# Where a batch's loads stand in the DMA queue: behind the stage's last store, with turns ahead of v

## The chip, the cores and the metric

The kernel runs on one core of one Trainium2 chip. The metric is device time in microseconds for one execution, inputs and outputs in HBM; the figure of a kernel is the median of several runs.

The names used below: TensorE (PE) does the matmuls, VectorE (DVE), ScalarE (ACT) and GpSimd (POOL) work element by element, SP only issues DMAs. Each engine works through its own program in order.

## The reference, cut to what matters

Attention over 8 batches, 8 heads, 576 positions, 64 dims, then a gated feed-forward block. Heads 0 to 3 ("plain") see the last 32 positions, heads 4 to 7 ("dilated") every fourth of the last 128.

```
scores = q @ k.T / sqrt(64)                 # per batch and head
plain:   0 <= i - j < 32
dilated: 0 <= i - j < 128 and (i - j) % 4 == 0
attn = softmax(scores where the mask holds)
x = (attn @ v), heads side by side          # 4608 tokens x 512
out = (gelu(x @ w_gate) * (x @ w_val)) @ w_out   # 512 -> 1536 -> 512
```

## The kernel before

**Tiles.** The 4608 tokens are cut into 9 chunks of 512. A chunk c has a gate stage (12 blocks of 128 hidden columns; a block is 4 matmuls with `wg` and 4 with `wv`, line 638) and an output stage (4 blocks of 128 tokens, 12 matmuls each, line 645). All these matmuls are 128x128 by 512 columns. Attention is spread between them: each batch has four pairs of heads, numbered n = 4 b to 4 b + 3, two plain and two dilated. Batches 2 and 3 begin with the dilated pairs, all others with the plain ones (`pair`).

**Lists of places.** The order on TensorE, and with it that on ScalarE and VectorE, is written out by hand, as words in the dictionaries `gates`, `outs` and `firsts`. A number is so many feed-forward matmuls. S is a pair's scores, P the exponential (ScalarE, line 510), M its mask (VectorE, 515), D the denominators, N the numerators (line 459 or 448), A or T and B the reciprocal (ScalarE 608 and 610, or VectorE 599 to 616), X the product that writes `xT` (VectorE, 629). `N22@1+D23@0` emits the two as one, split over quarters of the array (`emit_tiles`). The digit after @ is the PSUM window. `g` and `u` are a gate block's activation (803) and product (808). `e3@0` evicts block 3 of chunk 0 to an `osb` buffer on ScalarE (656) and stores it (660). `firsts` orders the first 16 matmuls of the gate stage.

**Loads.** A batch from 2 on is loaded in two steps on SP's queue. `load_first` (word F) brings q and k in float32 to the three parts of `stage`, and GpSimd casts them to `s16` (lines 221, 233). `load_rest` (word H) turns them by transposing DMAs into `qp`, `qd` and `dense` (line 275, "turns"), brings v to parts 1 and 2 of `stage`, and GpSimd spreads the keys out of `dense` (283, 291), copies the rest of q (L330) and casts v (264). Part 1 holds first k's plain heads, then v's plain heads; part 2 q's dilated heads, then v's dilated heads. A DMA that reuses a part waits for the cast that read it.

SP's program, in the order of the code, is therefore a row of loads with the stores between them. F2 and H2 stand in chunk 0's output list, and R (H3, F4, H4) in chunk 2's gate list. The others are issued by the loop at the end of the code: F3 ahead of chunk 1, F5 and H5 ahead of chunk 3, F6 and H6 ahead of chunk 4, F7 and H7 ahead of chunk 5. The word `e3@(c-1)`, the last store of a chunk's output, stands early in the next chunk's gate list, so on SP it is behind these loads. There are four `osb` buffers (`osbp`, bufs=4); block 3 of one chunk takes the buffer of block 3 of the chunk before.

The order of the transfers inside H:

```
turn qp; turn kdp (plain k)
load_v plain            # 4 transfers of 144 KB
turn qd; turn kdd (dilated k)
load_v dilated          # 4 of 128 KB and 4 of 16 KB
GpSimd: spread plain k, cast plain v, spread dilated k, copy rest of q, cast dilated v
```

Of the kernel before, what the change touches and what calls it, by code (L numbers as in the profile page):

```python
# [21 lines left out]
def kernel(  # L22
# [11 lines left out]
    B, H, S, D = q.shape  # L34
# [128 lines left out]
    def gated(ins):  # L163

        if "dma" in gate:
            tc.add_manual_dep(ins.ins, gate.pop("dma").ins.name, SYNC, reason="order of loads")
# [41 lines left out]
    def st_of(i):  # L208
        return stage[:, 1280 * i : 1280 * i + 1280]

    def load_plain(src, b, i):
        st = st_of(i).rearrange("p (k h d) -> p k h d", k=5, h=HK)
        for kb in range(4):
            nc.sync.dma_start(out=st[:, kb], in_=src[b, 0:HK, kb * P : kb * P + P, :].rearrange("h p d -> p h d"))
        for x in range(2):
            rest = src[b, x * HK : x * HK + HK, S - 64 : S, :].rearrange("h p d -> p h d")
            nc.sync.dma_start(out=st[64 * x : 64 * x + 64, 4], in_=rest)

    def cast_plain(t, i):
        for g in range(2):  # L220
            nc.gpsimd.tensor_copy(  # L221
                s16[:, 1280 * t + 640 * g : 1280 * t + 640 * g + 640].rearrange("p (k c) -> p k c", k=5),
                st_of(i).rearrange("p (k g c) -> p k g c", k=5, g=2)[:, :, g],
            )

    def load_dil(src, b, i):
        rows_ = src[b, HK:H, 0 : 4 * P, :].rearrange("h (p r) d -> p h (r d)", r=4)
        nc.sync.dma_start(out=st_of(i)[:, 0:1024].rearrange("p (h c) -> p h c", h=HK), in_=rows_)
# [9 lines left out]
    def load_v(b, i, plain):  # L238

        st = st_of(i)  # L240
        for g in range(2 * plain):
            for x in range(2):
                rows_ = v[b, 2 * g + x].rearrange("(j p) d -> p j d", p=64)
                dst = st[half_of(x, b and g), 576 * g : 576 * g + 576].rearrange("p (j d) -> p j d", j=NB2)
                gated(nc.sync.dma_start(out=dst, in_=rows_))  # L245
        for g in range(2 - 2 * plain):
            for x in range(2):
                half = st[half_of(x, g), 576 * x : 576 * x + 512]
                rows_ = v[b, HK + 2 * g + x, 0 : 4 * P].rearrange("(i p r) d -> p i (r d)", i=2, r=4)
                nc.sync.dma_start(out=half.rearrange("p (i c) -> p i c", i=2), in_=rows_)  # L250
        for g in range(2 - 2 * plain):
            for x in range(2):
                at = slice(576 * x + 512, 576 * x + 576)
                nc.sync.dma_start(out=st[half_of(x, g), at], in_=v[b, HK + 2 * g + x, S - 64 : S])

    def cast_v(dst, i, gs=(0, 1), swap=1, plain=1):

        st = st_of(i)[:, 0:1152].rearrange("p (e d) -> p e d", d=D)
        for g in gs:
            for x in range(2):  # L260
                y = x ^ (g * swap)
                src = g if plain else y
                at, of = (slice(NB2 * i, NB2 * i + NB2) for i in (g, src))
                nc.gpsimd.tensor_copy(dst[half_of(x), at, half_of(y)], st[half_of(x), of])  # L264

    def half_of(x, swap=0):
        y = x ^ (1 if swap else 0)
        return slice(64 * y, 64 * y + 64)
# [5 lines left out]
    def turn(dst, src):  # L274
        nc.sync.dma_start_transpose(out=dst, in_=src)
# [17 lines left out]
    def load_first(b):  # L293
        load_plain(q, b, 0)
        load_plain(k, b, 1)
        load_dil(q, b, 2)
        cast_plain(0, 0)
        cast_plain(1, 1)
        load_dil(k, b, 0)
        cast_dil(0, 2)  # L300
        cast_dil(1, 0)
# [17 lines left out]
    def load_rest(b):  # L319
        qp, qd, kp, kd, vp, vd = tiles["two", b] = views(b)  # L320
        turn(qp.rearrange("p g (k c) -> p (g k) c", c=P), s16[:, 0:1280])
        turn(kdp.rearrange("p g (k c) -> p (g k) c", c=P), s16[:, 1280:2560])
        load_v(b, 1, True)
        turn(qd.rearrange("p g r i -> p (g r) i")[:, :, 0:P], s16[:, 2560:3584])
        turn(kdd.rearrange("p g r i -> p (g r) i")[:, :, 0:P], s16[:, 3584:4608])
        load_v(b, 2, False)
        spread_plain(kp)
        cast_v(vp, 1)
        spread_dil(kd, kdp[:, :, S:640])
        nc.gpsimd.tensor_copy(qd[:, :, :, P:NCL], qp[:, :, S:640].rearrange("p g (i r) -> p g r i", r=4))  # L330
        cast_v(vd, 2, plain=0)

    def v_first(g):

# [449 lines left out]
    def run_program(c, words, mms, banks):  # L784
# [3 lines left out]
        for word in words.split():  # L788
# [47 lines left out]
            "u8 2 t9@5@0 t11@7@0 6 g9 u9 2 t12@4@1 t14@6@1 6 g10 u10 2 t13@5@1 t15@7@0 6 g11 u11"  # L836
        ),
        1: (
            "4 N7@0 e3@0 1 X7 1 G 8 g0 2 g1 1 u0 2 u1 2 g2 4 u2 4 g3 4 u3 4 g4 4 u4 4 g5 4 u5 4 g6 4 u6 4 g7 4 u7 "
            "4 g8 4 u8 4 g9 4 u9 4 g10 4 u10 4 g11 3"  # L840
        ),
        2: (
            "4 N11@1 e3@1 R 1 X11 G 7 g0 3 g1 u0 3 u1 3 g2 4 u2 4 g3 4 u3 4 g4 4 u4 4 g5 4 u5 4 g6 4 u6 4 g7 4 u7 "
            "4 g8 4 u8 4 g9 4 u9 4 g10 4 u10 4 g11 3"
        ),
        3: (
            "4 N15@0 e3@2 1 X15 G 7 g0 3 g1 u0 3 u1 3 g2 4 u2 4 g3 4 u3 4 g4 4 u4 4 g5 4 u5 4 g6 4 u6 4 g7 4 u7 4 "
            "g8 4 u8 4 g9 4 u9 4 g10 4 u10 4 g11 3"
        ),
        4: (  # L850
            "3 e3@3 M21 1 N19@0+D20@1 G 1 X19 6 T20 3 g0 2 N20@0+D21@1 g1 u0 1 u1 3 B20 1 g2 4 u2 3 T21 1 g3 4 u3 "
            "N21@1 1 X20 3 g4 1 B21 4 u4 3 X21 g5 4 u5 4 g6 4 u6 4 g7 4 u7 4 g8 4 u8 4 g9 4 u9 4 g10 4 u10 4 g11 "
            "3"
        ),
        5: (
            "G 2 N24@1 2 B24 e3@4 2 g0 2 X24 3 u0 2 g1 4 u1 4 g2 4 u2 4 g3 4 u3 4 g4 4 u4 4 g5 4 u5 4 g6 4 u6 4 "
            "g7 4 u7 4 g8 4 u8 4 g9 4 u9 4 g10 4 u10 4 g11 3"
        ),
        6: (
            "G 3 T28 3 e3@5 1 M31 N28@0+D29@1 g0 1 B28 4 u0 1 g1 1 T29 5 u1 N29@1 1 X28 1 g2 3 B29 4 u2 1 g3 2 "  # L860
            "X29 3 u3 3 g4 4 u4 4 g5 4 u5 4 g6 4 u6 4 g7 4 u7 4 g8 4 u8 4 g9 4 u9 4 g10 4 u10 4 g11 3"
        ),
        7: (
            "G 6 e3@6 2 g0 3 u0 2 g1 4 u1 4 g2 4 u2 4 g3 4 u3 4 g4 4 u4 4 g5 4 u5 4 g6 4 u6 4 g7 4 u7 4 g8 4 u8 4 "
# [2 lines left out]
    }  # L867
    outs = {
        0: (
            "V1 F2 S4@4 E P4 11 M4 S5@2 1 P5 3 D4@0 M5 S6@2 1 T4 P6 5 M6 e0@0 S7@2 1 P7 1 B4 3 e1@0 H2 1 M7 7 "  # L870
            "N4@1+D5@0 1 A5 X4 5 N5@0+D6@1 e2@0 1 A6 X5 5 N6@1+D7@0 1 A7 X6 1"
        ),
        1: (
            "1 u11 5 S8@0 1 E P8 10 e0@1 M8 1 S9@0 1 P9 3 D8@1 M9 S10@0 1 T8 P10 4 e1@1 1 M10 N8@0+D9@1 S11@0 B8 "
            "A9 3 X8 2 P11 4 e2@1 1 M11 N9@1+D10@0 1 A10 X9 7 N10@0+D11@1 1 A11 X10 1"
        ),
        2: (
            "1 u11 5 S12@2 1 E P12 10 e0@2 M12 1 S13@2 1 P13 3 D12@0 M13 S14@2 1 T12 P14 4 e1@2 1 M14 N12@1+D13@0 "
            "S15@2 B12 A13 3 X12 2 P15 4 e2@2 1 M15 N13@0+D14@1 1 A14 X13 7 N14@1+D15@0 1 A15 X14 1"
        ),  # L880
        3: (
            "1 u11 5 S16@0 1 E P16 10 e0@3 1 M16 S17@0 1 P17 3 D16@1 M17 S18@0 A16 4 N16@0+D17@1 e1@3 1 P18 X16 3 "
            "A17 1 M18 S19@0 3 P19 2 N17@0+D18@1 e2@3 M19 S20@0 A18 1 X17 4 P20 1 N18@1+D19@0 1 M20 A19 S21@0 1 "
            "X18 3 P21 1"
        ),
        4: (
            "1 u11 5 S22@2 1 E P22 10 e0@4 M22 1 S23@2 1 P23 3 D22@0 M23 S24@2 A22 4 N22@1+D23@0 e1@4 1 P24 X22 5 "
            "S25@2 T23 1 P25 N23@1 2 M24 2 e2@4 1 B23 3 M25 D24@0 2 X23 5 T24"
        ),
        5: (  # L890
            "D25@0 u11 2 T25 3 N25@1+S26@0 B25 1 E P26 3 X25 7 e0@5 M26 1 S27@0 1 P27 3 D26@0 M27 S28@0 1 T26 P28 "
            "4 e1@5 1 M28 N26@1+D27@0 S29@0 B26 1 P29 2 T27 4 N27@0+S30@0 X26 1 P30 3 B27 1 e2@5 1 D28@1+S31@0 "
            "M29 1 P31 1 M30 3 X27 3"
        ),
        6: "D30@0 u11 1 E A30 5 N30@1+D31@0 1 T31 5 X30 N31@0 e0@6 4 B31 4 X31 5 e1@6 12 e2@6 11",
    }
    firsts = {
        0: "000 100 002 102 001 101 010 110 012 112 011 111 003 103 013 113",
        1: "000 001 010 011 002 012 100 101 102 110 111 112 003 013 103 113",
        2: "002 003 012 013 000 010 102 103 100 112 001 011 101 113 110 111",  # L900
        3: "002 003 012 013 000 010 102 103 100 112 001 011 101 113 110 111",
        4: "100 101 102 000 001 002 010 011 012 110 111 112 003 013 103 113",
        5: "000 001 002 003 010 011 012 013 100 101 102 103 110 111 112 113",
        6: "000 001 002 003 010 011 012 013 100 101 102 103 110 111 112 113",
        7: "000 001 002 003 010 011 012 013 100 101 102 103 110 111 112 113",
    }
# [7 lines left out]
        run_program(c, outs.get(c, plain_out if c < NCH - 1 else plain_out[:-5] + "L"), out_list(c, banks), banks)  # L914

    for c in range(NCH):
        if 1 <= c and c + 2 < B and c != 2:
            load_first(c + 2)
            if c > 2:
                load_rest(c + 2)  # L920
        run_chunk(c)
# [1 line left out]
_INS = ['q', 'k', 'v', 'moe_w_gate', 'moe_w_val', 'moe_w_out']  # L923
# [26 lines left out]
```

## Time and profile before

| | us |
|---|---|
| median of 6 runs (339.62 to 343.67) | 341.29 |
| the profiled execution | 340.52 |
| its span, first to last instruction | 338.8 |
| busy: TensorE | 326.6 |
| busy: VectorE | 158.7 |
| busy: ScalarE | 157.7 |
| busy: GpSimd | 148.9 |
| feed-forward matmuls, one | 0.379 each by the page, 0.216 from start to start |

The page gives one execution. Matmuls overlap, so their lengths add up to more than the time; what one costs is the distance from its start to the next one's start. The granted clock of TensorE was 1.000 over the whole span. A timeline row has its start, its length, engine and line, and in brackets how long the engine had been idle and what ended the wait. SPq rows are DMA issues on SP; the time at which a transfer has landed is told apart from them.

### The profile page before, as it was taken

The page shows a single profiled execution, that of the slowest core. Times are in us where ns is not written, and L with a number is a line of the kernel's source. Part 1 is how long each engine was busy: PE and PEld are TensorE (multiplying, and loading weights), DVE is VectorE, ACT ScalarE, POOL GpSimd, SP SyncE. Part 2 cuts the span into 40 slices and gives each one's busy share as a digit, 9 for nine tenths or more (in the row PEclk, how much of TensorE's full clock was granted, in tenths as well). Part 3 has the DMA queues.
Part 4 walks back from the last instruction along what each step waited for, and adds up shares of the span by engine and source line. Part 5 has one row for each costly group of instructions (what it writes and reads, how often), then busy time and mean ns, then how long its engine had stood idle before and what let it go on. Part 6 is the DMA issues. An engine that isn't in the chain of part 4 may idle for free.

```text
span 338.8 us, 7043 instructions
## 1 busy us (share of the span) xinstructions
PE 326.6 (96%) x2780; PEld 163.8 (48%) x2780; DVE 158.7 (47%) x243; ACT 157.7 (47%) x235; POOL 148.9 (44%) x246
## 2 busy tenths in 40 slices
PE   7899999999969999999999999999999999999995
PEld 4654555444524455445544454445544544444443
DVE  6763554442624355443785365367844424304310
ACT  2663576434643458337853473345534343213321
POOL 8799787568235655726834842681000000000000
PEclk9999999999999999999999999999999999999999
DMA  8999995895789599779989938981100110020002
GB/s 184 190 181 182 204 186 128 222 218 151 167 268 196 134 227 182 196 182 233 190 198 214 196 136 176 256 156 64 64 0 3 63 64 0 0 93 33 0 31 96
DMA packets 109250, 47.96 MB, mean 142 GB/s; under 512 B 83872, under 2 KB 104736, under 8 KB 109216
## 3 DMA queue, kind: packets, MB, share of 16 engines
q1 hardware_dynamic: 97440, 39.99, 51.5%
q0 software_dynamic: 11216, 6.79, 14.0%
q10 hardware_dynamic: 560, 0.72, 0.8%
q8 instruction: 22, 0.36, 0.5%
q14 instruction: 12, 0.10, 0.1%
HBM read 37.75 MB, written 9.44 MB: 139 GB/s over the span
## 4 chain that ended last, share of the span: by engine, by line
PE 72%; DMA 15%; POOL 8%; SPq 2%; issue 1%; ACT 1%; DVE 0%; POOLq 0%; ACTq 0%
PE ps L638 42%; PE ps L645 23%; PE ps L448 4%; DMA wo<-in_moe_w_out_dram 4%; DMA stage<-in_v_dram 3%; PE ps L459 3%; DMA out_dram<-osb 2%; DMA u_all<-in_q_dram 2%; POOL v L264 2%; DMA stage<-in_k_dram 1%; DMA dense<-s 1%; SPq L245 1%; POOL v L206 1%; POOL wv L153 1%; POOL wg L153 1%
## 5 line engine op out<-in xcount | busy, mean ns | idle before, releaser
L808 DVE SCALAR_TENSOR_TENSOR u_all<-g,ps 128x512 f16<-128x512 f16 x108 | 73.8, 688 | 111.5 <-PE ps L638 101.6
L638 PE MATMUL ps<-xT,wv 128*128 128x512 f16 x432 | 112.7, 379 | 3.1 <-ACT osb L656 3.1
L638 PE MATMUL ps<-xT,wg 128*128 128x512 f16 x432 | 114.2, 379 | 0.4 <-ACT g L803 0.2
L803 ACT ACTIVATE g<-ps 128x512 f16<-128x512 f32 x108 | 64.0, 597 | 108.8 <-PE ps L638 108.6
L645 PE MATMUL ps<-wo,u_all 128*128 128x512 f16 x420 | 99.0, 379 | 0.0
L638 PEld LDWEIGHTS <-wg 128*128 128x128 f16 x432 | 41.6, 98 | 52.7 <-issue 4.6
L638 PEld LDWEIGHTS <-wv 128*128 128x128 f16 x432 | 42.2, 98 | 50.5
L645 PEld LDWEIGHTS <-u_all 128*128 128x128 f16 x420 | 38.0, 98 | 39.9
L264 POOL CAST v<-stage 64x576 f16<-64x576 f32 x60 | 40.8, 680 | 7.7 <-DMA stage<-in_v_dram 4.7
L629 DVE TENSOR_TENSOR xT<-ps,rb 128x576 f16<-128x576 f32 x32 | 29.8, 935 | 14.1 <-PE ps L459 7.9
L510 ACT ACTIVATE P<-ps 128x832 f16<-128x832 f32 (+1 forms) x32 | 26.7, 834 | 19.9 <-PE ps L448 14.6
L221 POOL CAST s<-stage 128x640 f16<-128x640 f32 x24 | 16.9, 733 | 38.1 <-DMA stage<-in_q_dram 24.1
L656 ACT ACTIVATE osb<-ps 128x512 f32<-128x512 f32 x34 | 20.2, 594 | 28.9 <-PE ps L645 24.4
L291 POOL COPY q<-dense 64x1152 f16<-64x1152 f16 (+1 forms) x28 | 20.3, 727 | 17.6 <-DMA dense<-s 17.1
L283 POOL COPY q<-dense 64x512 f16<-64x512 f16 x28 | 17.0, 633 | 4.3 <-DMA dense<-s 2.0
L233 POOL CAST s<-stage 128x512 f16<-128x512 f32 x24 | 14.7, 644 | 8.7 <-DMA stage<-in_q_dram 6.7
L515 DVE TENSOR_TENSOR P<-P,two_d 128x768 f16<-128x768 f16 x14 | 9.7, 694 | 15.8 <-ACT P L510 15.8
L608 ACT ACTIVATE lg<-ps 128x576 f32<-128x576 f32 x17 | 11.1, 651 | 7.5 <-PE ps L459 6.7
L448 PE MATMUL ps<-q 128*128 128x96 f16 (+2 forms) x225 | 13.2, 204 | 0.8 <-POOL q L330 0.8
L515 DVE TENSOR_TENSOR P<-P,two_p 128x832 f16<-128x832 f16 x14 | 9.5, 675 | 9.1 <-ACT P L510 8.9
L448 PEld LDWEIGHTS <-q 128*128 128x128 f16 x225 | 11.3, 98 | 4.7 <-issue 0.9
L459 PEld LDWEIGHTS <-v 64*64 64x64 f16 x400 | 9.2, 107 | 8.6 <-issue 6.9
(82 smaller groups left out, 207.2 us busy)
## 6 DMA issues: line engine op xcount, KB each, us to landing
out_dram<-osb SPq DMA_DIRECT2D x35, 256.0 KB, 2.3
stage<-in_v_dram SPq DMA_DIRECT2D x32, 144.0 KB, 3.9
stage<-in_v_dram SPq DMA_DIRECT2D x28, 128.0 KB, 3.0
stage<-in_q_dram SPq DMA_DIRECT2D x24, 128.0 KB, 3.1
stage<-in_k_dram SPq DMA_DIRECT2D x24, 128.0 KB, 2.9
stage<-in_q_dram SPq DMA_DIRECT2D x6, 512.0 KB, 4.4
stage<-in_k_dram SPq DMA_DIRECT2D x6, 512.0 KB, 5.4
wg<-in_moe_w_gate_dram POOLq DMA_DIRECT2D x6, 256.0 KB, 6.6
```

The lines of the kernel that those rows point to most:

```text
L264: nc.gpsimd.tensor_copy(dst[half_of(x), at, half_of(y)], st[half_of(x), of])
L291: nc.gpsimd.tensor_copy(out_, src[half].rearrange("p g (j c) -> p g j c", c=64))
L448: nc.tensor.matmul(o, lhs, rhs, start=st, stop=end, skip_group_check=True)
L459: nc.tensor.matmul(o[cols], lhs[rows, cols], rhs[rows], start=st, stop=end, skip_group_check=True)
L510: nc.scalar.activation(pt[:, 0 : src.shape[1]], src, AF.Exp, bias=0.0, scale=scale)
L515: nc.vector.tensor_tensor(pt, pt, mask, ALU.mult)
L629: nc.vector.tensor_tensor(dst, num, rb, ALU.mult)
L638: nc.tensor.matmul(ps[:, bank, :], w[:, kc, ns], xT[kc][:, tok], start=first, stop=end)
L645: nc.tensor.matmul(ps[:, bank, :], u_all[:, fc, tb * P : (tb + 1) * P], wo_t[fc // 4][:, fc % 4, :], start=(fc == 0), stop=(fc == NNB - 1),)
L656: nc.scalar.activation(osb, ps[:, bank, :], AF.Copy, bias=0.0, scale=1.0 / USCALE)
L803: nc.scalar.activation(g, ps[:, gate_banks(c, args[0])[0], :], AF.Gelu)
L808: nc.vector.scalar_tensor_tensor(u_all[:, nb, :], tiles.pop(("g", nb)), USCALE, val, ALU.mult, ALU.mult)
```

## The change

The loop at the end no longer issues loads. The words F3, F5 H5, F6 H6 and F7 H7 stand in the gate lists of chunks 1, 3, 4 and 5, each behind the word `e3` of the chunk before. In H, both dilated turns come ahead of all transfers of v, the dilated half of v ahead of the plain half, and on GpSimd both spreads come ahead of both casts of v, dilated v first. The lists `gates`, `outs` and `firsts` are redrawn for chunks 1 to 6, with small moves in chunk 0.

```diff
 def load_rest(b):
         turn(kdp..., s16[:, 1280:2560])
-        load_v(b, 1, True)
         turn(qd..., s16[:, 2560:3584])
         turn(kdd..., s16[:, 3584:4608])
-        load_v(b, 2, False)
+        for plain in (0, 1):
+            load_v(b, 2 - plain, plain)
         spread_plain(kp)
-        cast_v(vp, 1)
         spread_dil(kd, kdp[:, :, S:640])
         nc.gpsimd.tensor_copy(qd[:, :, :, P:NCL], ...)
         cast_v(vd, 2, plain=0)
+        cast_v(vp, 1)
 gates = {
         1: (
-            "4 N7@0 e3@0 1 X7 1 G 8 g0 2 g1 1 u0 2 u1 2 g2 ...
+            "3 N7@0 e3@0 F3 1 X7 1 G 8 g0 3 g1 u0 3 u1 2 g2 ...
         3: (
-            "4 N15@0 e3@2 1 X15 G 7 g0 ...
+            "4 N15@0 e3@2 F5 H5 1 X15 G 7 g0 ...
         4: (
-            "3 e3@3 M21 1 N19@0+D20@1 G 1 X19 6 T20 3 g0 2 N20@0+D21@1 g1 u0 1 u1 3 B20 1 g2 4 u2 3 T21 1 g3 ...
+            "2 e3@3 F6 H6 1 M21 1 G N19@1+D20@0 1 X19 6 T20 3 g0 2 N20@1+D21@0 g1 u0 1 u1 3 T21 1 g2 4 B20 N21@0 ...
         5: (
-            "G 2 N24@1 2 B24 e3@4 2 g0 2 X24 3 u0 2 g1 4 u1 4 g2 ...
+            "G 6 e3@4 F7 H7 B24 3 g0 1 N24@1+D25@0 u0 2 X24 1 g1 4 u1 N25@1 1 T25 3 g2 3 B25 3 u2 2 g3 1 X25 ...
 outs = {
         4: (
-            "... M23 S24@2 A22 4 N22@1+D23@0 e1@4 1 P24 X22 5 S25@2 T23 1 P25 N23@1 2 M24 2 e2@4 1 B23 3 M25 D24@0 2 X23 5 T24"
+            "... M23 S24@2 A22 4 N22@0+D23@1 P24 1 X22 1 e1@4 1 S25@2 1 P25 1 T23 5 M24 1 e2@4 2 M25 3 B23 N23@0+D24@1 1 T24 5 X23"
         5: (
-            "D25@0 u11 2 T25 3 N25@1+S26@0 B25 1 E P26 3 X25 7 e0@5 M26 1 S27@0 ... S28@0 1 T26 P28 ...
+            "1 u11 5 S26@0 1 E P26 10 e0@5 M26 1 S27@0 ... S28@0 A26 4 N26@1+D27@0 P28 ...
...
 for c in range(NCH):
-        if 1 <= c and c + 2 < B and c != 2:
-            load_first(c + 2)
-            if c > 2:
-                load_rest(c + 2)
         run_chunk(c)
```

## The prediction, written before the changed kernel was run

> **What bounds the kernel now.** I read the page first (busy time, chain), then the waits of TensorE alone, then the timelines of TensorE, ScalarE, SP and GpSimd around those waits. The page's first part and its chain:
>
> ```profile
> PE 326.6 (96%) x2780; PEld 163.8 (48%) x2780; DVE 158.7 (47%) x243; ACT 157.7 (47%) x235; POOL 148.9 (44%) x246
> PE 72%; DMA 15%; POOL 8%; SPq 2%; issue 1%; ACT 1%; DVE 0%; POOLq 0%; ACTq 0%
> ```
>
> TensorE is the bound, and its program is one fixed order, so any idle time of it past the start is lost for good. The waits of TensorE from 54 us to the end are three (total, times, longest):
>
> ```profile
> PE ps L638 <- ACT osb L656: 3.1, 1, 3.1
> PE ps L448 <- POOL q L330: 0.8, 1, 0.8
> PE ps L638 <- ACT g L803: 0.2, 1, 0.2
> ```
>
> All fall in one stretch, the output stage of chunk 1 and the first gates of chunk 2. TensorE's timeline there (start, length, idle before):
>
> ```profile
> 78.20 1.46 PE L645 MATMUL ps<-wo,u_all 128*128 128x512 f16 x6
> 79.67 0.34 PE L448 MATMUL ps<-q 128*128 128x96 f16 x4
> 80.81 0.33 PE L448 MATMUL ps<-q 128*128 128x80 f16 x5 [0.80 <-POOL q L330]
> ...
> 98.83 0.38 PE L638 MATMUL ps<-xT,wv 128*128 128x512 f16 x1 [3.07 <-ACT osb L656]
> ...
> 100.73 1.02 PE L638 MATMUL ps<-xT,wg 128*128 128x512 f16 x4 [0.24 <-ACT g L803]
> ...
> 118.00 1.46 PE L645 MATMUL ps<-wo,u_all 128*128 128x512 f16 x6
> ...
> 135.76 1.03 PE L638 MATMUL ps<-xT,wg 128*128 128x512 f16 x4
> ```
>
> From the first output matmul of chunk 1 (78.20) to the third gate block of chunk 2 (100.73) is 22.53 us. The same stretch one chunk on, with the same matmuls (118.00 to 135.76), takes 17.76. So 4.77 us are lost there and nowhere else. Why ScalarE was late, from its timeline and SP's:
>
> ```profile
> 93.75 0.69 ACT L610 ACTIVATE rb<-lg 128x576 f32<-128x576 f32 x1
> 98.18 0.60 ACT L656 ACTIVATE osb<-ps 128x512 f32<-128x512 f32 x1 [3.75 <-DMA out_dram<-osb]
> ...
> 90.52 0.45 SPq L228 DMA_DIRECT2D stage<-in_k_dram  x1
> 91.06 8.07 SPq L660 DMA_DIRECT2D out_dram<-osb  x5
> ```
>
> There are four `osb` buffers, so block 3 of chunk 1 needs chunk 0's block 3 stored. That store had its data at 58.6, but stood in SP's program behind `load_first(3)`: issued at 91.06, it took 7.0 us to land, behind the two 512 KB dilated loads.
>
> **The change part by part**, against this execution (340.52 us, span 338.8; the median of the six runs is 0.77 above).
>
> *Store ahead of the loads (batch 3).* SP's new order is two stores, then `load_first(3)`. The store is issued near 81.4; its neighbour issued at 80.84 landed in 3.6. So it lands by 85, 9 us before ScalarE asks (94.4). No wait takes its place: ScalarE evicts at 94.4, TensorE wants that bank at 95.6; and chunk 3, with the same words, runs without a gap. Gain 3.23 + 0.40 (starts 95.38 to 98.83 and 100.12 to 100.73, less 0.216 for a matmul each). A rule speaks against this: the Trainium skill, "DMA: Bandwidth & Descriptors", section "Anatomy of one DMA — SWDGE (gpsimd) path", fits a DMA as 2.0 us plus bytes over 436 GB/s, 2.6 us for 256 KB. By it the old store would have landed at 93.7, before 94.4, and this part would be worth nothing. It is fitted on the other kind of queue; the trace has 7.0 behind loads and 2.3 on an idle queue (issued 98.80). I take the trace.
>
> *Dilated turns ahead of v (batch 2).* S8 is dilated: its last operand is the copy L330, which ended at 80.8. Before it on GpSimd stood the cast of plain v (2.83, from 74.30) and a short wait for dense's dilated turn, landed 77.5. The two turns pass the four transfers of plain v on SP (2.7 us of issue, 69.78 to 72.45), the spreads pass its four casts on GpSimd. So the turns go out at about 69.8 and 71.3 and land by 76; the spreads end near 79.0, and S8 comes at 79.5. Gain 4.77 - 3.63 = 1.14. The dilated v lands by 80, its cast ends at 83, N8 comes at 86.
>
> *List of places.* Chunk 1's gate order brings g0 one matmul earlier; TensorE's start 60.52 to 60.94 was 0.2 too long, waiting for g0 (60.29 + 0.54). Gain 0.2. In chunks 4 and 5, N23, D24, N24, D25 alone (0.37 each, from 199.59 to 199.96 for N23) and N25+S26 as a pair (0.60) become N23+D24 and N24+D25 (0.57 each, as N22+D23 now) plus N25 (0.37) and S26 (0.34): 2.08 - 1.85 = 0.23. The Trainium skill, "TensorEngine Tiling (Array Packing)", section "Theoretical Speedup", allows up to 2x, a pair for the price of one, which would give 0.37; the rows decide. The lists keep the count of feed-forward matmuls in each stage. Wherever a normaliser moves, I followed the buffers: X24 has 7 matmuls (1.5 us) to end before N25 overwrites its window, against 0.5 for u0's end and 0.76 for itself; P18 ends within 0.1 of S19. I cost these at nothing, bounded by 0 and 0.5.
>
> *Store ahead of the loads of batches 5, 6, 7.* SP reaches these loads at 140.8, 169.1 and 201.8; the store put ahead has its data at 133.6, 169.7 and 204.4 before, some 5 us earlier in the new time. It adds one issue, 0.4. Behind the waiting store stand all 30 transfers of the batch (14 of the first load, 4 turns, 12 of v), and GpSimd's casts wait for those. The last two wait for ScalarE about as long as SP waits now for e3 of chunk 3 and e2 of chunk 4. Batch 7's first scores come at 233.2 while its plain keys are spread at 219.8: cover of 13 us.
>
> *Plain v last.* This is where something is late next. Batches 4 to 7 begin with plain pairs, and plain v is now their last transfer and last cast. GpSimd for batch 5:
>
> ```profile
> 158.54 2.59 POOL L291 COPY q<-dense 64x1152 f16<-64x1152 f16 x2 [1.67 <-DMA dense<-s]
> 161.20 3.04 POOL L264 CAST v<-stage 64x576 f16<-64x576 f32 x4
> ...
> 168.29 3.08 POOL L264 CAST v<-stage 64x576 f16<-64x576 f32 x4
> ```
>
> Plain v is cast at 164.2 now. In the new order, at unchanged SP times: turns until 158.3, dense's landed 162 to 163, spreads and L330 (2.9 to 3.2, 0.3) until 165.5 to 166.7, dilated v (2.83 to 3.08) until 168.3 to 169.8, N20's two casts of plain v (1.4) until 169.7 to 171.2. N20 stands at 171.94; less the 4.97 gained by then it comes at 167.0. But SP also moves up: it stood from 95.0 to 98.8 for the late eviction; that goes, less 0.5 for the store put ahead and what rings still full from the loads take. I take 2.9, which makes 166.8 to 168.3: a new wait of 0 to 1.3. I book 0.5. N24 (plain v about 195.5 against 200.8) and N28 have 5 us and more.
>
> Sum: 3.63 + 1.14 + 0.2 + 0.23 - 0.5 = 4.7. 340.52 - 4.7 = 335.8 for an execution like the profiled one, 336.6 for the median.
>
> **The rivals.** *Loads give it back (337.3 to 340.1):* if SP's lead at batch 5 is under 2 us, N20 waits 1.2 to 4. For: the DMA share from 60 to 172 us is mostly 7 to 9 tenths, so a backlog may eat the lead. Against: SP's 3.8 us stand is in the trace.
>
> *The store doesn't free the buffer in time, or S8 stays late (339.6 to 341.3):* that only one small gain arrives, if the eviction waits for another thing than its buffer. For: a wait for several semaphores is told by the last. Against: eviction start 98.18 and landing 98.09 agree.
>
> *Slower (343.5):* the buffer of plain v in `stage` is also that of the next batch's k. F's k transfers wait for the last cast, so each batch can hand delay to the next, and N20 pays. N20's data is ready at 169.7 to 171.2 with SP unmoved; the gain of 5.2 is gone at 172.2, and at 173.9 the kernel is over 0.5% slower, so SP must run about 3.5 later there. At 5 later: wait 7.3, net +2.1. Against: k is issued 4.3 us after the last v issue (112.97 to 117.27), plain v lands 3.5 to 4.9 after its own, which makes waits of 0 to 0.7 a batch, three batches before N20: 2 us at most, against a lead.
>
> **How the numbers follow.** Forecast 0.68, loads give back 0.15, no effect 0.08, slower 0.09. Half a per cent, 1.7 us, is what a measurement of this kernel can tell from none; the first two are faster: 0.83. The range, 335.0 to 339.8, takes the forecast with its unknowns (no wait at N20, pairs at the page's price) and the second case, and leaves out the last two.
>
> **What would show it.** Right: TensorE's list of waits loses the L656 and L330 rows; the stretch of chunk 1 takes about 17.8 us; the turn after F3 starts near 96 rather than 99.2; gates of chunk 1 have no 0.2 gap. Wrong: a wait of L459 on `v` L264 in chunk 4 of over 1.2 us, SP's k transfers waiting for L264, or the eviction of chunk 1's block 3 still waiting for a DMA.

## The result: 338.39 us, and the profile after

| | before | after |
|---|---|---|
| median, us | 341.06 (37 runs) | 338.39 (16 runs) |
| lowest to highest | 339.62 to 344.66 | 336.62 to 341.56 |
| the profiled execution | 340.52 | 336.62 |
| its span | 338.8 | 334.9 |

The ratio is 0.992, with a 95% interval of 0.9896 to 0.9943: 2.67 us faster, where 4.7 was forecast. The profiled execution of after gained 3.9, but it is one of the fastest of the 16; the median stands 1.8 above it, where before's stood 0.5 to 0.8 above its own. A ratio, here and below, leaves out executions that are over 1.5% above the fastest of their kernel; a median does not.

The page of after, first part and chain:

```profile
PE 326.0 (97%) x2791; PEld 163.6 (49%) x2791; DVE 157.4 (47%) x240; ACT 158.6 (47%) x237; POOL 149.1 (45%) x246
PE 79%; DMA 8%; POOL 6%; SPq 2%; ACT 1%; issue 1%; DVE 1%; POOLq 0%; DVEq 0%
```

TensorE does the same work, and it now stands for 79% of the chain instead of 72; the DMA share fell from 15 to 8. TensorE's waits in after from 54 us on (total, times, longest):

```profile
PE ps L459 <- POOL v L264: 0.8, 2, 0.5
PE ps L448 <- POOL q L291: 0.5, 1, 0.5
```

None of the three rows of before is left; both rows are new. The timeline of TensorE in after, over the stretch of chunk 1 that lost 4.77 us before:

```profile
77.97 1.46 PE L645 MATMUL ps<-wo,u_all 128*128 128x512 f16 x6
79.26 0.51 PE L448 MATMUL ps<-q 128*128 128x96 f16 x9
...
95.72 1.03 PE L638 MATMUL ps<-xT,wg 128*128 128x512 f16 x4
```

S8's nine matmuls (79.26) run in one piece, no row carries a wait in brackets, and 77.97 to 95.72 is 17.75 us, against 22.53 before. On ScalarE the eviction that had waited for its buffer now follows the reciprocal at once (92.96, before 98.18):

```profile
92.36 0.69 ACT L610 ACTIVATE rb<-lg 128x576 f32<-128x576 f32 x1
92.96 0.58 ACT L656 ACTIVATE osb<-ps 128x512 f32<-128x512 f32 x1
```

What came in its place is in chunks 3 and 4, on TensorE's timeline:

```profile
158.68 0.17 PE L459 MATMUL ps<-P,two_ones 64*64 64x16 f16 x1
159.34 0.54 PE L448 MATMUL ps<-q 128*128 128x96 f16 x9 [0.47 <-POOL q L291]
...
167.17 0.38 PE L638 MATMUL ps<-xT,wv 128*128 128x512 f16 x1
167.81 0.23 PE L459 MATMUL ps<-P,v 64*64 64x96 f16 x1 [0.27 <-POOL v L264]
168.54 0.23 PE L459 MATMUL ps<-P,v 64*64 64x96 f16 x1 [0.50 <-POOL v L264]
```

S20, the first scores of batch 5, waits for its plain keys, and N20 for its plain v. By the starts, and with 0.04 for a short matmul and 0.31 for the step from a gate matmul to a pair as elsewhere in this trace, S20 loses 0.6 and N20 1.0: 1.6 us. The two profiled executions can be compared stage by stage, by the start of the same feed-forward matmul. After starts chunk 1's output 0.24 earlier than before (0.2 of it is the gap at 60.94, gone), chunk 2's output 5.01 earlier, so chunk 1 gives the 4.77. Chunk 4's gates start only 4.46 earlier (S20), chunk 4's output 3.40 (N20), the last stage 3.56; the remaining 0.3 of the 3.9 lies behind the last of these matmuls.

What made the keys late shows on SP. Its timeline in after, behind `load_first(3)`, and then at the plain turns of batch 5:

```profile
94.05 3.57 SPq L275 DMA_TRANSPOSE q<-s  x1
97.71 2.29 SPq L275 DMA_TRANSPOSE dense<-s  x1
...
149.19 2.69 SPq L275 DMA_TRANSPOSE q<-s  x1
151.97 2.23 SPq L275 DMA_TRANSPOSE dense<-s  x1
```

The same two turns of batch 5 in before:

```profile
150.44 2.37 SPq L275 DMA_TRANSPOSE q<-s  x1
153.08 2.54 SPq L275 DMA_TRANSPOSE dense<-s  x1
```

SP reaches its first turn of batch 3 5.2 us earlier (94.05; before 99.22), but there the first two turns take 3.57 and 2.29 to issue, where before they took 1.39 and 1.46: 3.0 of the lead are gone at once. At F4 it is 1.7 (111.28 against 112.97), at F5 0.9 (139.89 against 140.83), at batch 5's turns 1.1 to 1.25. The prediction had 2.9 there.

While SP stood in before (95.0 to 98.8), the loads that it had issued ahead of that were still landing. GpSimd's cast of batch 3's last load, dilated k, in before and then in after:

```profile
97.52 1.17 POOL L233 CAST s<-stage 128x512 f16<-128x512 f32 x2 [0.21 <-DMA stage<-in_k_dram]
97.06 1.17 POOL L233 CAST s<-stage 128x512 f16<-128x512 f32 x2 [1.02 <-DMA stage<-in_k_dram]
```

That load lands only 0.5 earlier in after (97.00 against 97.47), and the first turn, started at 94.05, is through at 97.62. Its own data, plain q, had been cast by 89.8, so the turn did not wait for that. Batch 5 is alike: the last load lands at 153.84, the second turn is through at 154.20, the plain keys land at 156.6 (158.42 in before). Whether SP is held in such a row by the transfers ahead of it or by a semaphore is not shown, since the row's length has both.

### The profile page after: what moved, and what is told of

Its sections match the earlier page's. It is cut to its first block, busy times and chain, and to the rows that moved or that the text cites. A ratio compares the mean times of both kernels' runs of the same rounds, so it can differ in the third digit from the quotient of the medians.

```text
span 334.9 us, 7054 instructions
## 1 busy us (share of the span) xinstructions
PE 326.0 (97%) x2791; PEld 163.6 (49%) x2791; DVE 157.4 (47%) x240; ACT 158.6 (47%) x237; POOL 149.1 (45%) x246
## 4 chain that ended last, share of the span: by engine, by line
PE 79%; DMA 8%; POOL 6%; SPq 2%; ACT 1%; issue 1%; DVE 1%; POOLq 0%; DVEq 0%
PE ps L638 47%; PE ps L645 24%; DMA wo<-in_moe_w_out_dram 4%; PE ps L448 4%; PE ps L459 3%; DMA xT<-in_q_dram 2%; SPq L214 1%; DMA dense<-s 1%; POOL v L264 1%; DMA stage<-in_q_dram 1%; POOL q L291 1%; PE ps L669 1%; SPq L217 1%; POOL q L283 1%; POOL v L206 1%
## 5 line engine op out<-in xcount | busy, mean ns | idle before, releaser
L656 ACT ACTIVATE osb<-ps 128x512 f32<-128x512 f32 x34 | 20.1, 594 | 24.7 <-PE ps L645 24.1
L291 POOL COPY q<-dense 64x1152 f16<-64x1152 f16 (+1 forms) x28 | 20.7, 738 | 14.3 <-DMA dense<-s 13.8
```

Of the source, the lines that this page charges most:

```text
L291: nc.gpsimd.tensor_copy(out_, src[half].rearrange("p g (j c) -> p g j c", c=64))
L656: nc.scalar.activation(osb, ps[:, bank, :], AF.Copy, bias=0.0, scale=1.0 / USCALE)
```

## The experiments

Of the first four kernels one repeats the change, two cut it in pieces, and one turns an order in it round. They ran on one chip.

**again.** The changed kernel once more, for its spread.

> The changed kernel once more, beside the others on one chip. Theory A (the loads give part back: TensorE now waits for batch 5's keys at S20 and plain v at N20, 1.6 us in its profile, more in other executions): 2.5 to 3.0 us under the kernel before, and another profile shows waits of lines 448 and 459 on GpSimd in chunks 3 and 4 again, of 1 to 4 us in total. Theory B (the waits are peculiar to one profile, the rest is scatter of single executions): no such waits in this profile, or 4 us gained.

338.69 (12 runs, 336.25 to 341.18) against 341.3 (23 runs of before); ratio 0.9929 (0.9893 to 0.9965). Its profiled execution took 340.04. The waits of TensorE on attention's operands there:

```profile
PE ps L448 <- POOL q L291: 3.3, 1, 3.3
```

TensorE's timeline at S20 (start, length, idle before):

```profile
158.83 0.20 PE L459 MATMUL ps<-P,v 64*64 64x64 f16 x2
162.33 0.59 PE L448 MATMUL ps<-q 128*128 128x96 f16 x9 [3.31 <-POOL q L291]
162.74 2.32 PE L645 MATMUL ps<-wo,u_all 128*128 128x512 f16 x5
...
166.37 0.53 PE L448 MATMUL ps<-q 128*128 128x96 f16 x9
```

GpSimd's timeline has the spread of the plain keys, late by its DMA, and the page's second part (the granted clock in 40 slices, in tenths) a dip:

```profile
159.93 2.34 POOL L291 COPY q<-dense 64x1152 f16<-64x1152 f16 x2 [2.73 <-DMA dense<-s]
```

```profile
PEclk9999999999999999999799999999999999999999
```

The time is as expected (2.6 under before), and of the two waits the one on line 448 came, without that on line 459. The same kernel, and S20 waits 3.3 instead of 0.5: the dense turn was issued at 154.16 here (151.97 in the execution above) and landed at 159.81. And the wait costs more than itself. The five matmuls behind it take 2.32 us, 0.427 from start to start instead of 0.216, and the clock's row has a 7 there. From S20 to S21 the first profile of after has 2.47 us (159.34 to 161.81), this one 4.04: 1.57 lost to the clock. The S20 gap of 3.46 and these 1.57 make 5.0, against 1.6 of waits there; the difference of 3.4 is that of the spans (338.3 and 334.9).

**stores_only.** Before's lists and before's order of v; only the loads move behind the stores.

```diff
 # before's lists, words added behind the stage's last store:
-  1: "4 N7@0 e3@0 1 X7 ..."
+  1: "4 N7@0 e3@0 F3 1 X7 ..."       # 3: e3@2 F5 H5; 4: e3@3 F6 H6; 5: e3@4 F7 H7
 for c in range(NCH):
-        if 1 <= c and c + 2 < B and c != 2: load_first(c + 2) ...
         run_chunk(c)
```

> The kernel before with the words F3, F5 H5, F6 H6, F7 H7 behind e3, nothing else: old lists of places, plain v ahead of the dilated turns. Theory A: the eviction's wait of 3.6 us goes, S8's wait of 1.1 stays, and N20 doesn't wait, since plain v is cast early; 3.0 to 3.6 under the kernel before, so no slower than the whole change. Theory C (the eviction would wait for something else, the gain came with the turns): under 1 us gained.

337.04 (6 runs, 336.67 to 337.6), ratio 0.9879 (0.9842 to 0.9915): 4.3 us faster than before, and 1.65 faster than the whole change on the same chip. All waits of TensorE on attention's operands in its profile:

```profile
PE ps L448 <- POOL q L330: 0.8, 1, 0.8
PE ps L448 <- POOL q L283: 0.2, 1, 0.2
```

S8 still waits 0.8 and the 0.2 gap stays, so TensorE comes 1.3 later to S20 (160.01, against 158.72 without the wait in after); the plain keys are spread by 158.79, and there is no wait on L291 and none on v in chunk 4. All six executions kept a clock of 0.998 or more. The part alone is better than the whole by the medians, though the two intervals overlap a little. At full clock it is not: again's three executions at 1.0 have a median of 336.74. The rest of the change loses by the executions in which S20 waits long. This order is not free of that either: late14 below has it, and S20 waits 1.4 in its profile.

**turns_only.** Only the new order inside `load_rest`.

```diff
 def load_rest(b):
-        load_v(b, 1, True)
         turn(qd ...); turn(kdd ...)
-        load_v(b, 2, False)
+        for plain in (0, 1): load_v(b, 2 - plain, plain)
         spread_plain(kp)
-        cast_v(vp, 1)
         spread_dil(...); tensor_copy(qd ...); cast_v(vd, 2, plain=0)
+        cast_v(vp, 1)
```

> The kernel before with the new order inside H alone (turns ahead of v, dilated v ahead of plain v, spreads ahead of casts); loads stand where they stood. Theory A: S8's wait goes, 1.1 us gained; the eviction of chunk 1's block 3 still waits 3 to 4 us for the store, and N20 doesn't wait, since TensorE comes 3.6 us later than in the whole change: 340.0. Theory C: 3 us or more gained.

341.76 (12 runs), ratio 1.001 (0.9978 to 1.0041): nothing, where 1.1 was expected. TensorE's waits from 54 us on:

```profile
PE ps L638 <- ACT osb L656: 5.2, 2, 4.5
```

And its timeline behind the late eviction:

```profile
99.04 0.38 PE L638 MATMUL ps<-xT,wv 128*128 128x512 f16 x1 [4.46 <-ACT osb L656]
...
101.25 1.91 PE L638 MATMUL ps<-xT,wg 128*128 128x512 f16 x4
```

S8's row is gone, but the store that hands back the buffer is as late as before, so TensorE waits here by what it had won: it goes on at 99.04, before at 98.83. From 99.04 to 102.95 it then issues eleven matmuls in 3.91 us instead of 2.38: the granted clock was 0.50 from 99.9 to 103.2. The second wait in the list, 0.7 at 172.75, is of the same kind two chunks on: an eviction that had stood 2.2 for a store. The gain on S8 is real only once the eviction is free.

**plain_first.** The changed kernel, with plain v ahead of dilated v again from batch 4 on, in the transfers and in the casts.

```diff
-        for plain in (0, 1): load_v(b, 2 - plain, plain)
+        for plain in ((0, 1) if b < 4 else (1, 0)): load_v(b, 2 - plain, plain)
 # b >= 4: cast_v(vp, 1) ahead of cast_v(vd, 2, plain=0)
```

> The changed kernel, but in batches 4 to 7 (which begin with the plain pairs) plain v goes ahead of dilated v, in the transfers and in the casts; both turns still ahead of v. Theory A: N20's wait (1.1 us in the profile) goes, S20's (0.6) stays: 1 to 1.5 us under the changed kernel. Rival D (N20 waits because all of batch 5 is late, whatever is first in it): same as the changed kernel within 0.4 us, with a wait at S20 or at a later place of the same sum.

336.77 (6 runs), ratio 0.9864 (0.9822 to 0.9906). Its profile has one wait of TensorE from 54 us on, S20's, of 0.5 on L291. N20's wait on v is gone, as it should be with plain v cast first. The median is 1.9 under again's, where 1 to 1.5 was expected. On another chip below the same kernel did less well.

The next three ran on a second chip, against 340.8 for before.

**old_lists.** The changed kernel with before's lists, the load words put in: stores_only and turns_only together.

> The changed kernel with the lists of places of the kernel before (the words F and H placed as in the change, the new order inside H). Theory A' (the loads of batch 5 give part back, and where TensorE stands still for over about 3 us its clock is halved for some us after): N20 and S20 wait here as in the changed kernel, since the lists ahead of them do the same; 0.4 slower than the changed kernel by the pairs and the 0.2 gap, so 338.5 to 339.5. Rival E (the redrawn lists cause the new waits): no waits at S20 and N20, 337 or less.

338.75 (12 runs), ratio 0.9934 (0.99 to 0.9968), the same as again's. The 0.2 gap at 60.92 is there, and S20 waits in its profile, whose clock's row is the same as again's, with the 7 in the same slice:

```profile
PE ps L448 <- POOL q L291: 2.6, 1, 2.6
```

So the redrawn lists do not cause the wait, and by time they bring nothing that can be told from none. The granted clock was 0.50 from 162.8 to 166.2 here, though TensorE had stood for only 2.6 us.

**five_buffers.** Before, with one more output buffer and nothing else.

```diff
-    osbp = ctx.enter_context(tc.tile_pool(name="osbp", bufs=4))
+    osbp = ctx.enter_context(tc.tile_pool(name="osbp", bufs=5))
```

> The kernel before with five osb buffers in place of four; no order changed. Theory A': block 3 of chunk 1 then takes block 2's old buffer, whose store landed at 84, so the eviction doesn't wait although its store is still issued behind F3: 3.6 us and what the halved clock costs gone, S8's wait of 1.1 stays, clock 1.0 in nearly all executions; 337.0 to 337.8, as with the stores moved. Rival (the order on SP itself matters, the loads after it too): 338.5 or more.

337.17 (6 runs, 336.87 to 337.87), ratio 0.9893 (0.9865 to 0.9921), all clocks 0.998 or more. The store stays behind the loads and lands as late (98.05; 98.09 in before); the eviction of chunk 1's block 3 no longer needs its buffer and follows the reciprocal at once:

```profile
94.42 0.58 ACT L656 ACTIVATE osb<-ps 128x512 f32<-128x512 f32 x1
```

Its waits of TensorE on attention's operands are those of stores_only (0.8 and 0.3), and there is none on L656.

**ahead.** plain_first with five buffers, `load_first(5)` moved up into chunk 2's output, and the plain turns of batch 5 moved up too, ahead of S15.

> The changed kernel with plain v first in batches 4 to 7, five osb buffers, and batch 5's first load (F5) and plain turns issued in chunk 2's output list, ahead of stores of that chunk instead of behind all four. Theory A': the plain keys of batch 5 land about 2 us earlier, S20 waits in no execution, clock 1.0 throughout: 1 us under the version with plain v first alone (336.8), so 335.2 to 336.0. Rival F (the DMA engines are full, so order on SP moves nothing): same as plain v first, with S20 waiting 0.5 or more.

368.35. The turn took the place of batch 3's queries before S15 had read them, so S15 computes with batch 5's and waited 30.8 us for them. This run tells nothing of the loads.

**late10 and late14.** A measurement of the clock by itself: stores_only, with ten or fourteen activations whose result nobody reads on ScalarE ahead of g6 of chunk 7. They hold TensorE up once, in a stage where nothing else does.

```diff
+  elif kind == "Z":          # word Z10 or Z14 ahead of g6 in chunk 7
+      lg = nrm.tile([P, S], F32, tag="lg", bufs=1)
+      for _ in range(args[0]): nc.scalar.activation(lg[:, 0:CH], ones, AF.Gelu)
```

> The kernel before with only the stores moved (337.0, clock 1.0), and ten activations of 512 columns that write a buffer nobody reads, put on ScalarE ahead of g6 of chunk 7: a late ScalarE in a stage without attention, so TensorE stands still for about 10 x 0.59 - 1.13 - 1.95 = 2.8 us. Theory G (the clock is halved only by an idle time of more than about 3 us): 2.8 slower than without them, 339.8, all matmuls after the wait 0.216 apart, clock 1.0. Rival (any wait halves it, or none): over 341.5, or the same price per idle us in both kernels.

> The same with fourteen such activations: TensorE stands still for about 5.2 us. Theory G: the matmuls after the wait run 0.427 apart for some 3 us, about 8 of them, so 5.2 + 1.7 = 6.9 slower than without: 343.9, clock 0.995. Rival (idle time costs only itself): 342.2, clock 1.0.

On a third chip, against 341.94: late10 took 342.07 (10 runs; ratio 0.9993, 0.9957 to 1.0028), late14 346.82 (4 runs; 1.0136, 1.0051 to 1.0221). TensorE's timeline at the added wait in late10's profile:

```profile
286.86 1.86 PE L638 MATMUL ps<-xT,wg 128*128 128x512 f16 x4 [3.32 <-ACT g L803]
288.52 1.80 PE L638 MATMUL ps<-xT,wv 128*128 128x512 f16 x4
290.16 1.03 PE L638 MATMUL ps<-xT,wg 128*128 128x512 f16 x4
```

Eight matmuls take 3.30 from 286.86 to 290.16, and 1.73 at full clock: 1.57 on top of the wait, as in again. Both expectations were missed: 339.8 and 343.9 stood there. In late10 the idle was to be 2.8 with a full clock; it was 3.3, and eight of the ten executions had a clock of 0.995 or less (341.58 to 344.17), while the two at 1.0 took 340.15 and 340.2. How long TensorE stood in the others is not on record. late14's idle was 6.0 instead of 5.2, the clock was halved in all four, and S20 waits there too, for 1.4.

No one length of idle parts the cases. The clock was halved behind 2.6 us in old_lists and not behind 3.1 in before.

**ahead2 and plain_first2.** The misplaced turn mended: plain_first, five buffers, `load_first(5)` at the start of chunk 2's output, batch 5's plain turns right behind S15. Beside it plain_first again.

```diff
-  bufs=4
+  bufs=5
 outs 2:
-  "1 u11 5 S12@2 ... B12 S15@2 A13 ..."
+  "1 u11 F5 5 S12@2 ... B12 S15@2 Y5 A13 ..."     # Y5: turns qp and kdp of batch 5
 gates 3:
-  "4 N15@0 e3@2 F5 H5 ..."
+  "4 N15@0 e3@2 H5 ..."
```

> As 'ahead', but the plain turns of batch 5 come behind S15, the last reader of the q that they overwrite (in 'ahead' they came before it, so that S15 waited for them and read batch 5's q in place of batch 3's: that kernel left a pair wrong, and its time tells nothing of the order of loads). Theory A': batch 5's plain keys land 2 us earlier, S20 doesn't wait, clock 1.0 in nearly all executions: 335.2 to 336.3. Rival F (the DMA engines are full, so order on SP moves nothing): as plain v first, S20 waits 0.5 us or more and some executions lose the clock.

> The version with plain v first again, beside 'ahead2' on one chip: 336.4 to 337.2 by both theories, with S20 waiting 0.3 to 3 us in its profile.

On a fourth chip, against 341.81: ahead2 took **335.53** (6 runs, 335.14 to 336.65), ratio 0.9831 (0.9788 to 0.9874), the lowest of all. Its interval lies apart from again's, but overlaps those of stores_only, plain_first and five_buffers. TensorE has no wait of 0.2 us or more from 54 us to the end. It is just enough: GpSimd's spread of the plain keys ends at 158.77 and S20 starts at 158.83 (L458 is line 448 of the other kernels). GpSimd's timeline and TensorE's:

```profile
156.21 2.56 POOL L291 COPY q<-dense 64x1152 f16<-64x1152 f16 x2 [3.05 <-DMA dense<-s]
```

```profile
158.83 0.54 PE L458 MATMUL ps<-q 128*128 128x96 f16 x9
```

In after the same spread ended at 159.28, so all moves of loads brought 0.5 at this place, in one execution each. But all six executions agree, where the changed kernel's differ, and had a clock of 0.998 or more. Three things were changed at once here (the buffer, the first load, the turns); which of them does it is not shown.

plain_first2 took 338.43 (334.53 to 341.82), where 336.4 to 337.2 was expected; its ratio is 0.9857 (0.9795 to 0.9918). Its profiled execution, the slowest (341.82), has a wait of 3.8 at S20, and the granted clock was 0.50 from 161.8 to 168.6, twice as long as in again. The order of v thus removes N20's wait but not S20's, which is 0.5 in one execution and 3.8 in the next.

## Why the prediction was right or wrong

TensorE's lead over before's profiled execution, us, by the start of the same matmul:

| | chunk 1's output | chunk 2's output | chunk 4's gates | chunk 4's output | last stage |
|---|---|---|---|---|---|
| after | 0.24 | 5.01 | 4.46 | 3.40 | 3.56 |
| again | 0.07 | 4.84 | -0.10 | -0.01 | 0.15 |
| stores_only | 0.32 | 3.79 | 3.79 | 3.79 | 3.79 |
| ahead2 | 0.36 | 5.13 | 4.97 | 4.66 | 4.83 |

The first two columns differ by 4.77 in after, again and ahead2 alike: the gain of chunk 1 came in full each time, and what the executions differ by is lost at S20 and N20, ahead of the third and fourth column.

*What bounds it, and the eviction (3.63): right.* The stretch takes 17.75, as forecast. five_buffers shows that it was the buffer's reuse: with a fifth buffer the gain is there although the store is as late as before. The rule that put this part at nothing was wrong here: 2.6 us by it, 7.0 by the trace.

*S8 (1.14): right as a wait, worth nothing alone.* S8's last operand came at 77.4 + 0.3 instead of 80.5 + 0.3 (sooner than the 79 booked), and its row is gone. turns_only, 1.001, shows what the sum had not said: this gain exists only behind the freed eviction (its interval leaves out the 1.1).

*The gap and the lists (0.2 + 0.23): the gap went, and the pairs brought a little less.* From chunk 4's output to the last stage the lead grows by 0.16 in after and again and 0.17 in ahead2, and by nothing in stores_only. By time the sum can't be told from none: old_lists, which has neither, is 0.9934 against again's 0.9929.

*"I take 2.9, which makes 166.8 to 168.3 ... I book 0.5": the term that was mis-sized.* SP's lead at batch 5's turns was 1.1 to 1.25 in the first profile, and in again the turn came 0.9 later than before. Of the 5.2 us that SP gained up to its first turn of batch 3, 3.0 went at once into longer rows of the two turns there; the last load ahead of them landed at 97.00, only 0.5 earlier than before. SP's stand had mostly run beside those landings. N20 lost 1.0, twice the booking; and S20, 8 us ahead of it and served by the same loads, was booked nothing and lost 0.6 in one execution and 3.5 in another. One number does both. In before the plain keys were spread by 161.13 (158.54 + 2.59) and S20 came at 163.80; less the 4.97 it comes at 158.83. With 2.9 of lead the keys are there by 158.2. With the 1.85 that came (159.28) they are 0.45 late, and the wait was 0.47. The first rival named this mechanism ("a backlog may eat the lead"), but at N20 instead of S20. Against stores_only, again is 1.65 slower by the median although it has the gain on S8, so what came back is more than the turns and the lists brought.

*A term that was in neither sum: the clock after a long wait.* A wait of 3.3 us on TensorE cost about 1.6 more, in 512-column matmuls at 0.427. The Trainium skill, "TensorE: Matmul & The Clock Gate", section "Part 1: The HAM clock gate (the "warmup" mystery)", has it: after an idle window of some 3.4 us, free-running, the array gets half of its pulses until it has been busy for as long, 426.7 ns for 512 columns against 215.7. The traces agree on both figures and on the time at half clock (3.4 us in again and old_lists, 6.8 in plain_first2), but not on the idle: 2.6 us were enough in old_lists. One such event of 3.4 us at half clock is 1.7 of 338, a mean clock of 0.995, and the executions sort by it: of before's 23 in the first call, eight at 0.998 or more have a median of 340.2, ten at 0.993 to 0.995 one of 341.4, five at 0.988 one of 343.9. For after it is 337.9 (nine of the 16 at 0.998 or more) and 339.6 (six near 0.995). In the first call again has 336.7 (three at full clock), 338.7 (seven near 0.995) and 341.1 (two near 0.99). So the clock widens both kernels; at full clock they stand 3.4 apart in that call and 2.3 with the first runs of after, still less than 4.7, so it does not by itself explain the missing 2 us. The prediction's +0.77 from profile to median was too small for a kernel whose wait varies from 0.5 to 3.3.

*The rivals.* That the change does nothing is out, and that it is slower too. "Loads give it back" (337.3 to 340.1) is what happened: 2.0 of the 4.7 did not arrive, and the measured 338.39 lies in the stated range only because that range took in most of this rival; the sum itself was not met. The likeliest case should have been this one.

*Open.* Why the same kernel's turn of batch 5 is issued 2.2 us later in one execution than in another; GpSimd's first cast of batch 5's q waited for its data until 146.22 in the one and 148.47 in the other, so it begins ahead of the turns, in the transfers. No run here takes that apart. Nor is it settled what idle halves the clock: 3.1 us did not in before's profile, 2.6 did in old_lists'.

## What to carry to other kernels

When an engine waits for a buffer, look at who hands it back: here a store queued behind loads, and one more buffer did the same as the reordering, with less to go wrong. Before you book a wait taken from the bounding engine, walk to every later place where it meets the same loads, the first one above all, and ask how much lead is left there; a sender that is no longer held up may only come to wait for its own loads. Here a wait of 2.6 us or more on TensorE mostly cost some 1.6 us beside itself (once more, and once nothing); read the clock of each execution before comparing medians.

## What the runs showed of the hardware

- Half clock behind a wait: 0.427 us from start to start for 512 columns, for about eight matmuls, after 3.3 us of idle (late10, again) and in all executions after 6.0 (late14). After 2.6 us too (old_lists, granted clock 0.50 from 162.8 to 166.2), and not after 3.1 (before).
- The row of one transposing DMA on SP was 1.3 us long, and 2.2 to 3.9 for the two turns behind the loads of batches 3 to 6 in after.
- Freed of 3.8 us of standing, SP was only 1.7 ahead at F4, 0.9 at F5 and 1.1 to 1.25 at batch 5's turns. The last load issued ahead of that stand landed only 0.5 earlier.
